# A two-layer expert kernel: bounds, probes and tally of the second layer's search re-ordered, and the first expert's weight splits moved past search phases

## The chip, the cores and the metric

The kernel runs on one core of a Trainium2 chip. The metric is the device time of one execution in microseconds (us); the median of the runs before the change is 927.05 us (three runs, 924.12 to 927.51). Besides these, one execution was profiled; it took 930.23 us, and its span from the first to the last instruction is 928.2 us.

## What is computed

Attention over q, k and v (batch 4, 12 heads, 448 tokens, width 64) gives 1792 rows of 768 numbers. Two expert layers follow. The first sends each row to its best expert by a gate. The second one is the subject here: every (row, expert) pair has a logit, the pairs are taken from the largest logit down, and an expert that has 224 rows is full.

```python
def _moe2_ref(x, w_gate, w1, w2) -> np.ndarray:
    N, D = x.shape
    E = w_gate.shape[1]
    cap = N // E
    logits = x @ w_gate
    flat = logits.flatten()
    order = np.argsort(-flat)
    assigned = -np.ones(N, dtype=np.int64)
    counts = np.zeros(E, dtype=np.int64)
    for idx in order:
        tok, e = (int(idx) // E, int(idx) % E)
        if assigned[tok] >= 0 or counts[e] >= cap:
            continue
        assigned[tok] = e
        counts[e] += 1
        if (assigned >= 0).all():
            break
    out = np.zeros((N, D), dtype=np.float32)
    for e in range(E):
        mask = assigned == e
        h = np.maximum(x[mask] @ w1[e], 0.0)
        out[mask] = h @ w2[e]
    return out.astype(np.float32)
```

## The kernel before

Matrix products are made of three TensorE (PE) products each: every fp32 operand is split into a high part (ScalarE copies it into fp32r) and a low part (VectorE subtracts), and high-high, high-low and low-high are added up.

The first layer's last block ends in `moe1` with lines 491 to 525. There the second layer's logits, all but the last block's, are loaded into `L`; `tail0` to `tail3` copy the last block's output, transpose it (`tail1`, whose second half VectorE copies into `yb`, L238), multiply it with the gate (`tail2`, L243) and transpose the logits back (`tail3`, L249, L250). Between them VectorE finds the smallest and largest logit (L503, L504), PE transposes the two numbers (L508), and VectorE makes 40 thresholds from them (L512 to L517). `warm` puts idle matmuls into PE's queue.

The second layer (`moe2`) doesn't sort. It finds one expert at a time: the generator `phases()` runs `search(p)` and `assign(p)`, and each `yield` ends a phase. One expert has 15:

- Phase 1 takes each row's best logit and compares it with 40 thresholds (`probe`, L680: 14 x 40 results a partition, `t_g`). Phases 2, 4, 6 and 8 count the rows over each threshold with 14 small matmuls (L723) and compare the counts with the capacity (L724, L728). Phases 3, 5 and 7 add up the comparisons with one matmul (L736), narrow the thresholds (L739) and probe again.
- Phase 9 takes the final threshold and tallies the rows over it by expert (L743 to L746, `tally`, `owned`). Phase 10 adds the tally up (L624), lowers the capacities and picks the full expert, whose number lets the SP queue load its weights (L753 to L767). Phases 11 to 15 make the list of its 224 rows: a running count, an offset matmul (L774), one-hot tables (L783 to L787), 14 matmuls on them (L791), the index matmul (L797) and the index list `idx` (L800). GpSimd then gathers the rows (`gather`, L849).

The order in which the queues get their work is written out in the program's text. Expert 0's search runs alone (`finish(0)`). After that `go(n)` runs n phases at once, while `turn`, called after each half of an up product and each pair of a down product, runs one when a countdown (the numbers `YY`) has run out. The first expert's head (L931 to L955) runs phases 1 to 5 of expert 1 between warm matmuls, then `take` transposes the rows, and then the loop over k = 0 to 5 makes the first four hidden slices (`up4`, L898), splits a chunk of w1 for k + 2 (`split`, L841 and L842) and calls `go(1)`:

```python
        for k in range(KD):
            if k:
                go(1)
            if k + 2 < KD:
                split(0, k + 2)
            up4(k, 0, 2)
            if k in (2, 3):
                go(1)
            up4(k, 2, 4)
```

So the loop holds phases 6 to 12. The next loop (L957 to L965) makes slices 4 to 7 (`up`, L891, 18 matmuls a slice), with `relu` (L903, L904) and the splits of the eight chunks of w2 in the order 0, 4, 1, 5, 2, 6, 3, 7. The down product (`down`, L914) follows in 16 pairs of slices; its first pair needs chunks 0 and 1, its second 2 and 3, its fourth 6 and 7. Weights come in a ring of eight buffers `raw`. The other seven experts run the same loops, with the next search in the turns.

## Time and profile before

| What | Value |
|---|---|
| median of three runs | 927.05 us |
| the profiled execution: its own time | 930.23 us |
| the profiled execution: its span | 928.2 us |
| PE busy | 872.0 us (94% of the span) |
| VectorE busy | 596.1 us (64%) |
| ScalarE busy | 478.7 us (52%) |
| GpSimd busy | 178.7 us (19%) |
| mean granted TensorE clock | 0.986 of full speed |

A busy share is a mean over stages that have different limits. In the trace the first layer ends near 582 us, the first search of the second layer lasts to about 603 us, the first expert's head to about 640 us, and the other experts fill the rest.

### The profile page before, as it was taken

The page shows a single profiled execution, that of the slowest core. Times are in us where ns is not written, and L with a number is a line of the kernel's source. Part 1 is how long each engine was busy: PE and PEld are TensorE (multiplying, and loading weights), DVE is VectorE, ACT ScalarE, POOL GpSimd, SP SyncE. Part 2 cuts the span into 40 slices and gives each one's busy share as a digit, 9 for nine tenths or more (in the row PEclk, how much of TensorE's full clock was granted, in tenths as well). Part 3 has the DMA queues.
Part 4 walks back from the last instruction along what each step waited for, and adds up shares of the span by engine and source line. Part 5 has one row for each costly group of instructions (what it writes and reads, how often), then busy time and mean ns, then how long its engine had stood idle before and what let it go on. Part 6 is the DMA issues. An engine that isn't in the chain of part 4 may idle for free. (4 is left out here: it accounts for less than half of the span.)

```text
span 928.2 us, 18427 instructions
## 1 busy us (share of the span) xinstructions
PE 872.0 (94%) x6380; PEld 726.8 (78%) x6380; DVE 596.1 (64%) x1749; ACT 478.7 (52%) x1042; POOL 178.7 (19%) x235
## 2 busy tenths in 40 slices
PE   7999999967999999798999999889999999999987
PEld 5666666646787887676888888468989999999987
DVE  7779898867463526738621241788888798875641
ACT  7777777765464526637722242035544354545541
POOL 6644444010111211110212120101011011011001
PEclk9999999989999999989999999999999999999999
DMA  7453537148374616837731111177575575666810
GB/s 177 120 150 103 149 102 227 51 129 295 127 275 134 237 54 216 337 109 284 281 99 35 54 38 41 58 262 227 190 234 187 161 235 177 220 195 195 263 51 30
DMA packets 73888, 151.05 MB, mean 163 GB/s; under 512 B 30481, under 2 KB 38705, under 8 KB 73714
## 3 DMA queue, kind: packets, MB, share of 16 engines
q1 hardware_dynamic: 67602, 123.33, 40.9%
q0 software_dynamic: 6112, 25.71, 8.4%
q8 instruction: 71, 1.16, 0.5%
q14 instruction: 103, 0.84, 0.3%
HBM read 130.34 MB, written 18.67 MB: 161 GB/s over the span
## 5 line engine op out<-in xcount | busy, mean ns | idle before, releaser
L206 PE MATMUL pU<-w1h,xx 128*128 128x512 f32 x336 | 119.1, 412 | 4.3 <-ACT yr L229 2.5
L891 PE MATMUL w<-xh,w1h 128*128 128x224 f32 x360 | 102.1, 284 | 0.7 <-ACTq L979 0.7
L891 PE MATMUL w<-xl,w1h 128*128 128x224 f32 x360 | 99.2, 276 | 1.2 <-issue 1.2
L891 PE MATMUL w<-xh,w1l 128*128 128x224 f32 x360 | 98.9, 275 | 0.6 <-DVEq L979 0.6
L1147 ACT ACTIVATE p<-p,nm 112x112 f32<-112x112 f32 (+2 forms) x192 | 98.8, 518 | 0.7 <-DVE nm L1139 0.7
L1139 DVE CUSTOM_DVE_ANT_0 p<-s,msk 112x112 f32<-112x112 f32 (+2 forms) x192 | 76.1, 445 | 23.6 <-PE s L1136 23.3
L914 PE MATMUL w<-w2h,hh 128*112 128x384 f32 x256 | 89.7, 350 | 0.1
L914 PE MATMUL w<-w2h,hl 128*112 128x384 f32 x256 | 86.5, 338 | 0.0
L914 PE MATMUL w<-w2l,hh 128*112 128x384 f32 x256 | 86.0, 336 | 0.0
L206 PEld LDWEIGHTS pU<-w1h,xx 128*128 128x128 f32 x336 | 63.7, 190 | 21.9 <-ACT yr L229 3.1
L891 PEld LDWEIGHTS w<-xl,w1h 128*128 128x128 f32 x360 | 69.1, 192 | 1.5 <-issue 1.4
L891 PEld LDWEIGHTS w<-xh,w1h 128*128 128x128 f32 x360 | 69.0, 192 | 1.4 <-ACTq L979 0.9
L891 PEld LDWEIGHTS w<-xh,w1l 128*128 128x128 f32 x360 | 69.1, 192 | 0.7 <-DVEq L979 0.7
L176 DVE TENSOR_TENSOR w2l<-raw,w2h 128x768 fp32r<-128x768 f32 x64 | 58.2, 954 | 17.1 <-ACT w2h L175 14.6
L224 PE MATMUL pY<-w2h,hh 128*128 128x384 f32 x224 | 60.7, 353 | 7.7 <-ACT w1h L175 5.0
L842 DVE TENSOR_TENSOR w2l<-raw,w2h 128x768 fp32r<-128x768 f32 x64 | 60.9, 952 | 8.6 <-ACT w2h L841 8.4
L206 PE MATMUL pU<-w1l,xx 128*128 128x512 f32 x168 | 66.1, 398 | 0.2 <-DVE w1l L441 0.2
L903 ACT ACTIVATE hh<-w 128x224 fp32r<-128x224 f32 x64 | 22.9, 358 | 82.0 <-PE w L891 56.3
L842 DVE TENSOR_TENSOR w1l<-raw,w1h 128x1024 fp32r<-128x1024 f32 x48 | 58.1, 1220 | 9.6 <-ACT w1h L841 9.4
L176 DVE TENSOR_TENSOR w1l<-raw,w1h 128x1024 fp32r<-128x1024 f32 x42 | 49.7, 1220 | 22.0 <-ACT w1h L175 22.0
L224 PE MATMUL pY<-w2h,hl 128*128 128x384 f32 x224 | 58.6, 343 | 1.0 <-DVE hl L217 1.0
L224 PE MATMUL pY<-w2l,hh 128*128 128x384 f32 x224 | 58.8, 345 | 0.0
(327 smaller groups left out, 2041.5 us busy)
## 6 DMA issues: line engine op xcount, KB each, us to landing
raw<-in_moe_w_dram SPq DMA_DIRECT2D x96, 512.0 KB
raw<-in_moe_w_dram SPq DMA_DIRECT2D x128, 384.0 KB
vt<-in_v_dram SPq DMA_DIRECT2D x48, 112.0 KB
qr<-in_q_dram SPq DMA_DIRECT2D x23, 224.0 KB
kr<-in_k_dram SPq DMA_DIRECT2D x23, 224.0 KB
xs<-xr SPq DMA_DIRECT2D x4, 1120.0 KB
xs<-xr SPq DMA_DIRECT2D x4, 238.0 KB
y<-yr SPq DMA_DIRECT2D x1, 384.0 KB
```

Of the source, the lines that this page charges most:

```text
L176: (on or nc.vector).tensor_sub(l, r, h.bitcast(F32))
L206: nc.tensor.matmul(pU[half], a[:, k], w[:, k, cs], start=(m == 0), stop=(m == 17))
L224: nc.tensor.matmul(pY[g][:, :384], a[:, k], w[:, k, g * 384:(g + 1) * 384], start=(k == 0 and t == 0), stop=(k == KF - 1 and t == 2))
L842: V.tensor_sub(l, r, h.bitcast(F32))
L891: nc.tensor.matmul(u, w[:, k, fs], x[:, k], start=(k == 0 and n == 0), stop=(k == KD - 1 and n == 2))
L903: A.activation(hh[:, f], u, AF.Relu)
L914: nc.tensor.matmul(y, a[:, f, g * G2:(g + 1) * G2], w[:, f, hf * 384:(hf + 1) * 384], start=(f == 0 and n == 0), stop=(f == KF - 1 and n = ...
L1139: nc.vector.tensor_tensor_reduce(P[u, h][:, o:o + w], s[h][:, :w], msk[:, S - w:], scale=-0.125, scalar=3.0e38, op0=OP.add, op1=OP.min, ac ...
L1147: nc.scalar.activation(p, p, AF.Exp, bias=RS[u, "m"][:, h, i:i + 1], scale=-1.0, accum_out=RS[u][:, h, i:i + 1])
```

## The change

Five places are edited. (1) At the end of the first layer the minimum and maximum are taken ahead of two other operations and written into `mn2`; the copy of `yb` follows them, and on PE the gate product of the last block stands ahead of the transposes of the bounds. (2) In expert 0's search, and there alone, the probe is two operations over 7 of 14 columns each, and the one-hot table stands ahead of the first probe. (3) The tally of phase 9 compares and multiplies in one operation, ahead of `asg` and `fl`; in phase 10 `mem` stands ahead of `ei`, and `fl` behind. Two warm matmuls behind expert 0's 14 index matmuls are gone. (4) An index list of zeros and one gather with it are issued ahead of expert 0's search. (5) In the head's loop `go(1)` is called at k = 4 and 5 and once behind the loop; it was called seven times.

```diff
-        V.tensor_tensor_reduce(d, d, hp, scale=-1.0, scalar=0.0, op0=OP.mult, op1=OP.add, accum_out=tk)
-        V.tensor_scalar(oi, iok[:, :NB], tk, None, op0=OP.is_equal)
-        V.tensor_reduce(d[:, 0:1], L, axis=AX.XY, op=OP.min)
-        V.tensor_reduce(d[:, 1:2], L, axis=AX.XY, op=OP.max)
-        tail1()
-        warm(2)
-        for n in range(2):
-            nc.tensor.transpose(pU[0][:, n * 128:n * 128 + 128], d[:, n:n + 1].to_broadcast([128, 128]), ident)
-        tail2()
+        V.tensor_reduce(mn2[:, 0:1], L, axis=AX.XY, op=OP.min)
+        V.tensor_reduce(mn2[:, 1:2], L, axis=AX.XY, op=OP.max)
+        tail1()
+        V.tensor_tensor_reduce(d, d, hp, scale=-1.0, scalar=0.0, op0=OP.mult, op1=OP.add, accum_out=tk)
+        V.tensor_scalar(oi, iok[:, :NB], tk, None, op0=OP.is_equal)
+        warm(2)
+        tail2()
+        for n in range(2):
+            nc.tensor.transpose(pU[0][:, n * 128:n * 128 + 128], mn2[:, n:n + 1].to_broadcast([128, 128]), ident)
         warm(2)
...
-        def probe():
+        def probe(parts=1):
 
-            V.tensor_tensor(T["g"][:, :, :TH], T["mm"][:, :, None].to_broadcast([128, PT, TH]),
-                            thr[:, None, :].to_broadcast([128, PT, TH]), op=OP.is_ge)
+            for i in range(parts):
+                s = slice(i * PT // parts, (i + 1) * PT // parts)
+                n = s.stop - s.start
+                V.tensor_tensor(T["g"][:, s, :TH], T["mm"][:, s, None].to_broadcast([128, n, TH]),
+                                thr[:, None, :].to_broadcast([128, n, TH]), op=OP.is_ge)
...
-                probe()
                 V.tensor_tensor(T["oh"], L, T["mm"][:, :, None].to_broadcast([128, PT, E]), op=OP.is_equal)
+                probe(2)
...
-                    probe()
+                    probe(1 if p else 2)
+            V.scalar_tensor_tensor(T["ao"], T["mm"][:, :, None].to_broadcast([128, PT, E]), thr[:, 0:1], T["oh"],
+                                   op0=OP.is_ge, op1=OP.mult)
+            with nc.allow_low_precision("small whole numbers"):
+                V.tensor_reduce(T["rab"], T["ao"].rearrange("p i e -> p e i"), axis=AX.X, op=OP.add)
             V.tensor_scalar(T["asg"], T["mm"], thr[:, 0:1], None, op0=OP.is_ge)
             V.tensor_scalar(T["fl"][:, 2:3], T["fl"][:, 2:3], float(PT), None, op0=OP.not_equal)
-            tally()
...
             V.tensor_reduce(T["em"], T["full"], axis=AX.X, op=OP.min)
-            V.tensor_scalar(T["fl"][:, :2], T["fl"][:, :2], 0.0, None, op0=OP.not_equal)
+            V.tensor_scalar(T["mem"], own, T["em"], None, op0=OP.is_equal)
             V.tensor_scalar(T["ei"], T["em"], 8.0, 7.0, op0=OP.add, op1=OP.min)
             EV[p] = nc.values_load(T["ei"][0:1, 0:1], engines=[SP], min_val=0, max_val=E - 1)
-            V.tensor_scalar(T["mem"], own, T["em"], None, op0=OP.is_equal)
             with nc.allow_low_precision("small whole numbers"):
                 V.tensor_reduce(T["rt"], T["mem"], axis=AX.X, op=OP.add)
+            V.tensor_scalar(T["fl"][:, :2], T["fl"][:, :2], 0.0, None, op0=OP.not_equal)
             yield YY[4]
...
             V.tensor_scalar(T["ev"], t[:16, :NA], float(N), None, op0=OP.min)
-            if p == 0:
-                warm(2)
             yield YY[9]
...
-        def gather(p):
-            for g in range(2):
+        def gather(p, n=2):
+            for g in range(n):
...
         reset()
+        nc.gpsimd.memset(idx[0], 0)
+        gather(0, 1)
         finish(0)
...
         for k in range(KD):
-            if k:
-                go(1)
             if k + 2 < KD:
                 split(0, k + 2)
             up4(k, 0, 2)
-            if k in (2, 3):
+            if k > 3:
                 go(1)
             up4(k, 2, 4)
+        go(1)
         ahead[0] = 1
```

How this moves instructions shows on VectorE, in three places. The first is the end of the first layer, before the change (`xg` holds `d`, `hp`, `tk` and `oi`; ISA is the multiply with a sum, L501):

```order
L500 SCALAR_TENSOR_TENSOR xg_3364<-xg_3364 128x128
L501 ISA xg_3364<-xg_3364 128x128
L501 ISA xg_3364 128x1
L502 TENSOR_SCALAR xg_3364<-iok_78,xg_3364 128x14
L503 TENSOR_REDUCE xg_3364<-L_82 128x1
L504 TENSOR_REDUCE xg_3364<-L_82 128x1
L238 COPY yb_3371<-pB1_3393 128x256
L512 TENSOR_REDUCE srch0_84<-pU0_3394 128x1
```

and with the change:

```order
L500 SCALAR_TENSOR_TENSOR xg_3364<-xg_3364 128x128
L501 TENSOR_REDUCE xg_3364<-L_82 128x1
L502 TENSOR_REDUCE xg_3364<-L_82 128x1
L238 COPY yb_3371<-pB1_3393 128x256
L504 ISA xg_3364<-xg_3364 128x128
L504 ISA xg_3364 128x1
L505 TENSOR_SCALAR xg_3364<-iok_78,xg_3364 128x14
L512 TENSOR_REDUCE srch0_84<-pU0_3394 128x1
```

The copy of `yb` has moved past three instructions, and they stand between it and the first operation on the transposed bounds (L512).

The second place is the head's loop, behind the three low parts of the gathered rows; before (`w1l` is the split of a w1 chunk, L724 and L728 belong to the even phases, L739 to the odd ones):

```order
L842 TENSOR_TENSOR w1l_23636<-raw2_90,w1h_23635 128x1024
L724 ISA t_d_23675,t_mx_23676<-gp_24062,t_capm_23667 40x8
L724 ISA t_mx_23676 40x1
L728 TENSOR_SCALAR t_ok_23677<-t_mx_23676 40x1
L732 ISA t_ao_23679,t_fl_23681<-t_oh_23673 128x112
L732 ISA t_fl_23681 128x1
L842 TENSOR_TENSOR w1l_23636<-raw3_91,w1h_23635 128x1024
L739 SCALAR_TENSOR_TENSOR srch3_87<-gp_24095,steps_23658,t_base_23696 128x40
L680 TENSOR_TENSOR t_g_23674<-t_mm_23670,srch3_87 128x14x40
L718 TENSOR_TENSOR t_col_23702<-srch3_87,steps_23658 128x1
L719 TENSOR_SCALAR t_base_23696<-iok_78,steps_23658,t_col_23702 128x40
L842 TENSOR_TENSOR w1l_23636<-raw4_92,w1h_23635 128x1024
```

and with the change:

```order
L846 TENSOR_TENSOR w1l_23636<-raw2_90,w1h_23635 128x1024
L846 TENSOR_TENSOR w1l_23636<-raw3_91,w1h_23635 128x1024
L846 TENSOR_TENSOR w1l_23636<-raw4_92,w1h_23635 128x1024
L846 TENSOR_TENSOR w1l_23636<-raw5_93,w1h_23635 128x1024
L727 ISA t_d_23675,t_mx_23676<-gp_24117,t_capm_23667 40x8
L727 ISA t_mx_23676 40x1
L731 TENSOR_SCALAR t_ok_23677<-t_mx_23676 40x1
L735 ISA t_ao_23679,t_fl_23681<-t_oh_23673 128x112
L735 ISA t_fl_23681 128x1
L742 SCALAR_TENSOR_TENSOR srch3_87<-gp_24147,steps_23658,t_base_23696 128x40
L683 TENSOR_TENSOR t_g_23674<-t_mm_23670,srch3_87 128x14x40
```

The last four splits of w1 stand in one run ahead of phase 6; before, the phases stood between them.

The third place is the end of the w2 splits; before, the one-hot tables of phase 13 (`t_a`, `t_b`) stood ahead of the first of the eight (chunk 0, `raw6`):

```order
L783 TENSOR_TENSOR t_a_23692<-t_ab_23691,ioi_23640 128x210
L785 TENSOR_TENSOR t_b_23693<-t_ab_23691,ioi_23640 128x224
L787 TENSOR_TENSOR t_a_23692<-t_a_23692,tok_23642 128x210
L904 SCALAR_TENSOR_TENSOR hl_23639<-w_24046,hh_23634 128x224
L842 TENSOR_TENSOR w2l_23638<-raw6_94,w2h_23637 128x768
L904 SCALAR_TENSOR_TENSOR hl_23639<-w_24212,hh_23634 128x224
L842 TENSOR_TENSOR w2l_23638<-raw2_90,w2h_23637 128x768
```

and with the change:

```order
L846 TENSOR_TENSOR w2l_23638<-raw1_89,w2h_23637 128x768
L783 COPY t_col_23702<-gp_24314 128x1
L785 SCALAR_TENSOR_TENSOR t_si_23690<-t_cum_23687,t_col_23702,t_mem_23686 128x14
L786 TENSOR_SCALAR t_ab_23691<-t_si_23690 128x14
L787 TENSOR_SCALAR t_ab_23691<-t_si_23690 128x14
L908 SCALAR_TENSOR_TENSOR hl_23639<-w_24291,hh_23634 128x224
L846 TENSOR_TENSOR w2l_23638<-raw5_93,w2h_23637 128x768
L789 TENSOR_TENSOR t_a_23692<-t_ab_23691,ioi_23640 128x210
L791 TENSOR_TENSOR t_b_23693<-t_ab_23691,ioi_23640 128x224
L793 TENSOR_TENSOR t_a_23692<-t_a_23692,tok_23642 128x210
L798 TENSOR_SCALAR t_ev_23694<-gp_24346 16x15
```

Phase 12 now stands ahead of the last w2 split (chunk 7, `raw5`) and phase 13 behind it. On PE the 14 index matmuls of phase 14 stand behind the third pair of the down product, and the index matmul of phase 15 behind the fourth.

## Rows read from the trace of the kernel before

**Rows 1.** Busy time by stretch: start:end, length, busy time (count) of PE, PEld, DVE, ACT, POOL, granted clock, DMA.
```profile
612.70:626.80 14.10, 12.39 (x105) 11.41 (x105) 12.16 (x46) 5.41 (x8) 0.00 (x0) 0.88 0.68 239
...
626.80:640.00 13.20, 13.20 (x113) 12.73 (x111) 11.71 (x31) 7.60 (x15) 2.52 (x6) 1.00 0.70 213
...
640.00:888.00 248.00, 245.27 (x2012) 231.50 (x2011) 191.20 (x552) 116.66 (x187) 27.24 (x26) 1.00 0.64 205
```

**Rows 2.** Timeline of PE around the bounds: start, us, engine, line, operation, idle before.
```profile
582.32 0.93 PE L233 MATMUL pB<-ident,yr 128*128 128x128 f32 x6 [0.72 <-ACT yr L229]
...
583.75 0.50 PE L508 MATMUL pU<-ident,xg 128*128 128x128 f32 x2
...
584.18 0.42 PE L243 MATMUL pA<-hb,wg 128*32 128x128 f32 x8
...
584.74 0.60 PE L488 MATMUL pU<-iob,before 128*128 128x512 bf16 x2
```

**Rows 3.** Timeline of VectorE around the bounds.
```profile
583.79 0.41 DVE L238 COPY yb<-pB 128x256 f32<-128x256 f32 x1
...
584.36 0.29 DVE L512 TENSOR_REDUCE srch<-pU 128x1 f32<-128x128 f32 x1 [0.15 <-PE pU L508]
...
585.67 0.18 DVE L250 TENSOR_REDUCE l2c<-pA 128x8 f32<-128x32 f32 x1
```

**Rows 4.** Timeline of VectorE in one round of the first search and at its end.
```profile
589.94 0.74 DVE L680 TENSOR_TENSOR t_g<-t_mm,srch 128x560 bf16<-128x560 f32 x1
...
590.60 0.15 DVE L718 TENSOR_TENSOR t_col<-srch,steps 128x1 f32<-128x1 f32 x1
...
591.29 0.16 DVE L724 CUSTOM_DVE_ANT_0 t_d<-gp,t_capm 40x8 f32<-40x8 f32 x1 [0.19 <-PE gp L723]
...
601.61 0.17 DVE L792 TENSOR_SCALAR t_ev<-gp 16x15 f16<-16x15 f32 x1 [0.59 <-PE gp L791]
```

**Rows 5.** Timeline of PE in the same round and at the same end.
```profile
590.74 0.51 PE L723 MATMUL gp<-t_oh,t_g 128*40 128x8 bf16 x14 [0.16 <-DVE t_g L680]
...
591.18 0.60 PE L594 MATMUL w<-iob,before 128*128 128x512 bf16 x2
...
602.04 0.21 PE L797 MATMUL gp<-t_ev,sel 16*112 16x15 f16 x1
```

**Rows 6.** Timeline of GpSimd: the second layer's first and second gathers.
```profile
603.59 1.13 POOL L849 DMA_INDIRECT xg<-y,idx  x1 [16.80 <-issue]
...
633.41 1.22 POOL L849 DMA_INDIRECT xg<-y,idx  x1 [27.23 <-DVE hl L904]
```

**Rows 7.** Timeline of PE in the first expert of the second layer.
```profile
626.81 0.28 PE L891 MATMUL w<-xh,w1h 128*128 128x224 f32 x1
...
629.71 0.27 PE L891 MATMUL w<-xl,w1h 128*128 128x224 f32 x1
...
638.96 0.34 PE L914 MATMUL w<-w2h,hh 128*112 128x384 f32 x1
...
641.00 0.51 PE L723 MATMUL gp<-t_oh,t_g 128*40 128x8 bf16 x14 [0.82 <-DVE t_g L680]
```

**Rows 8.** Timeline of VectorE in the first expert of the second layer.
```profile
620.33 0.26 DVE L739 SCALAR_TENSOR_TENSOR srch<-gp,steps,t_base 128x40 f32<-128x40 f32 x1 [0.27 <-PE gp L736]
...
621.83 1.22 DVE L842 TENSOR_TENSOR w1l<-raw,w1h 128x1024 fp32r<-128x1024 f32 x1
...
625.58 0.16 DVE L777 COPY t_col<-gp 128x1 f32<-128x1 f32 x1 [1.19 <-PE gp L774]
...
627.14 0.38 DVE L904 SCALAR_TENSOR_TENSOR hl<-w,hh 128x224 fp32r<-128x224 f32 x1
...
637.53 0.95 DVE L842 TENSOR_TENSOR w2l<-raw,w2h 128x768 fp32r<-128x768 f32 x1
```

**Rows 9.** Busy time by stretch around two idle times of PE, columns as in rows 1.
```profile
622.00:625.00 3.00, 3.00 (x16) 3.00 (x16) 2.36 (x14) 0.00 (x0) 0.00 (x0) 0.50 0.36 112
...
889.00:893.00 4.00, 1.75 (x11) 1.38 (x11) 1.35 (x2) 1.09 (x2) 0.00 (x0) 1.00 0.27 82
```

More of the change, by code (lines that the diff above doesn't have):

```diff
@@ L494, in moe1 @@
         V = nc.vector
-        d, hp, rh, oi, tk = xg[:, :128], xg[:, 128:256], xg[:, 256:256 + NB * E], xg[:, 512:512 + NB], xg[:, 640:641]
+        d, hp, rh, oi, tk, mn2 = xg[:, :128], xg[:, 128:256], xg[:, 256:256 + NB * E], xg[:, 512:512 + NB], xg[:, 640:641], xg[:, 648:650]
         V.tensor_copy(tk, sin)
```

## The prediction, made before the changed kernel was run

> **What bounds the kernel now.** I read the page's busy shares first (TensorE, PE, has work in 94% of the span), then the busy times by stretch, then the timelines of PE, VectorE and GpSimd where the change acts. From 640 us on PE is busy for 245.27 of 248 us [rows 1]: nothing there absorbs or adds, so a shift of the first expert's down product reaches the end of the kernel whole. The change acts between 582 and 640 us. In the head's loop (612.7 to 626.8) PE is busy for 12.39 of 14.10 us at a granted clock of 0.88, VectorE for 12.16; in the stretch behind it PE for all of 13.20 us and VectorE for 11.71 [rows 1]. The reader should see two engines that are both nearly full: VectorE is idle for only 1.94 + 1.49 = 3.43 us of 27.3. Shortening PE's loop helps only until VectorE decides.
>
> **End of the first layer (edit 1).** Before, the transposes of the bounds start at 583.75 and the gate product (0.42 us) follows at 584.18 [rows 2]; VectorE's first reduction of the bounds (L512) waits 0.15 us for PE and then runs on without a wait up to the copy of the logits (L250, 585.67) [rows 3]. Now the gate product comes first. It needs the copy of `yb` (L238, at 583.79, 0.41 us [rows 3]), whose source is done at 582.32 + 0.93 = 583.25 [rows 2]. Before, the copy stood behind four operations that are now behind it or already done; now it can take 583.3 to 583.7, and the gate product starts at about 583.75, where the bounds started. It holds PE for 0.56 us (584.18 to 584.74, its start to the next operation's [rows 2]). The bounds follow 0.56 us later, and since L512 to L250 have no slack, so does the search: **+0.56**. Were the logits the last thing to come, the earlier gate product would give back at most 584.18 - 583.75 = 0.43. As L250 shows no wait, I take +0.56 and keep -0.43 as the other end.
>
> **First search (edits 2 and 3).** A probe of 560 elements takes 0.74 us, with the next operation 0.66 us after its start [rows 4]; an operation of 224 elements takes 0.38 with the next one 0.30 on [rows 8]. Between them lies 280 elements: 0.44, the next 0.36 on. Two halves take 0.72 of VectorE's time, not 0.66: +0.06 a round. PE's 14 counting matmuls take 0.44 (590.74 to 591.18 [rows 5]) after the whole probe; now seven of them run beside the second half, and 0.22 is left behind it, 0.22 - 0.06 = 0.16 earlier. VectorE waited 0.19 us for them (591.29 [rows 4]), which with its 0.06 leaves at most 0.13. Three rounds give **-0.4**; the first probe gives nothing, because the one-hot table, which the matmuls need too, moved ahead of it. The ends are -0.5 (0.16 x 3) and +0.25 (four times 0.06, if the matmuls wait for both halves; the order of the program puts their second wait at the eighth).
>
> A rule speaks against halves. The Trainium skill, page "VectorE: DVE Perf Modes", section "The TRN2 errata — SBUF-src ops pay a fixed extra latency per instruction", says that many small tiles pay a fixed cost each, and gives some 150 cycles at 0.96 GHz. By that four more instructions would be an estimated +0.6 us, and the search would come out 0.5 worse than in my sum. The rows show a start-to-start fixed part of about 0.06 (the pair 224/0.30 and 560/0.66), because the next instruction starts before the last one ends.
>
> The fused tally takes out one operation of VectorE and changes no dependence that PE waits on: 0 (to -0.28, the length of such an operation in the loop). In phase 10 `mem` goes ahead of `ei`: -0.05 (to -0.14); the expert's number comes 0.06 later, and its loads have slack. The two warm matmuls stood between the index matmuls and the index product: `ev` ends at 601.61 + 0.17 = 601.78 [rows 4] and the product starts at 602.04 [rows 5]; it can start at 601.84: **-0.2**. Together the first search comes to +0.56 - 0.4 - 0.05 - 0.2, about **-0.1**.
>
> **Gather of row zero (edit 4).** GpSimd is idle for 16.80 us ahead of the real gather at 603.59, whose issue takes 1.13 us [rows 6]. The extra gather is one more such issue in that idle time, into a buffer that the real one overwrites, so it hides; cost without cover would be 1.13. If a first issue is slower than later ones, it could take that off the real gather: 603.59's 1.13 is no longer than the second one's 1.22 [rows 6], so I take 0 (-0.3 to +1.1).
>
> **The head's loop (edit 5).** Four calls of a phase leave the loop; it keeps phases 6, 7 and 8. PE's 1.71 us without work go, and the 3 us at clock 0.50 (622 to 625 [rows 9]) cost about 1.7 that a full clock saves; the wait inside phase 8 is kept (+0.4), the small matmuls of four phases go (-0.6): the loop ends about **3.6 us earlier**, at 623.2 instead of 626.8. That isn't a gain yet, because the same VectorE work must still be done. I follow its chain. Slice 4's 18 matmuls (0.11 each: 27 from 626.81 to 629.71 make 2.90 [rows 7]) end at 625.2; the first `hl` and the phases that now come with the turns follow at about 625.6. From there on VectorE has, in one run: phase 9 1.50 (620.33 to 621.83); seven pairs of `hl` and split, 0.30 + 0.87 each, 8.2; phases 10 and 11 1.42 (end of the split at 621.83 + 1.14 to 625.58, less the wait of 1.19); phases 12 and 13 1.56 (625.58 to 627.14) [rows 8]. That is 12.7, and the last split ends at 638.3; before it ended at 637.53 + 0.95 = 638.48 [rows 8]. **So of 3.6 us, 0.2 survive on VectorE.**
>
> PE pays the rest by waiting: about 1.8 us ahead of the second pair of the down product, for the split of chunk 3 (done near 635.5, wanted near 633.7), and 1.3 ahead of the 14 index matmuls of phase 14, which need the tables of phase 13 that now stand behind the last split. Then come phase 14 (0.54), the fourth pair of slices (1.05, half of 638.96 to 641.0 without its wait [rows 7]) and the index product with its wait (0.35): the fifth pair starts near 640.3. Before, the point that answers to it is the end of the counting matmuls at 641.00 + 0.44 = 641.4 [rows 7], which holds phase 2 of expert 2 (0.55 with its wait shortened) that now comes later. The gain is 641.4 - 0.55 - 640.3 = 0.6: **-0.6** (0 to -3.6).
>
> The gather for expert 1 moves from 633.41 to about 641, the searches of all later experts run four turns later; the gathered rows are wanted only at expert 1's start, far behind.
>
> **Sum.** -0.1 and -0.6: -0.7. The profiled execution took 930.23 us, so 929.5 by its own time. It lies 3.18 above the median of 927.05; against that median I forecast **926.3**.
>
> **The rivals.** *The loop's gain is kept* (0.22): VectorE's idle 3.43 us close up, because its operations run closer together when they stand in a run, and both pairs come as early as PE's loop allows. -3.6 and -0.1: 923.4. For it: the splits overlap PE work in either order. Against it: 638.3 against 638.48 above.
>
> *Slower: the clock falls* (0.20). PE has worked without a pause from 626.8 to 640 [rows 1]; in the new order it waits for about 3.1 of the 4.6 us from 633.7 to 638.3. Such a thinned stretch inside the loop left a clock of 0.50 over 622 to 625 [rows 9]. If the same follows here, some 3.4 us of products run at half rate, worth 1.7: -0.7 + 1.7 = +1.0, 928.0. [...] Against it: from 889 to 893 PE is busy for 1.75 of 4 us at clock 1.00 [rows 9]. The Trainium skill, page "TensorE: Matmul & The Clock Gate", section "What's actually happening", says that the throttled clock is the default and that activity releases it; by that the fall is what idling invites, and the two stretches of rows 9 bear it out once and not the other time.
>
> *Expert 1 starts late* (0.06): its gather sits at 641 behind GpSimd's own work, and four chunk loads behind the late number; PE then waits some 4 us at the next head: 931.
>
> **How the numbers follow.** The forecast has 0.50, with 924.7 to 928.7 as its own range (the ends of the first layer's and of the probe's terms, and 1.0 for the median of a few runs). The range reaches from somewhat below the first rival (923.4 less the 1 us) to somewhat above the second (928.0 and 1.7): 922.4 to 929.7. About 0.5%, 4.6 us, is what a measurement of this kernel can tell from no change; that is under 922.4 or over 931.7. Half of the first rival (0.11: it lies 1 us from that bound) and 0.02 of the forecast's lower end make faster 0.13; the third with a trace of the second makes slower 0.07; 0.80 stays.
>
> **What would show it.** Right: L512 starts near 584.9; the second probe half overlaps counting matmuls; the index product starts within 0.1 us of `ev`; the loop ends 3 to 4 us earlier; PE waits for `w2l` at the second pair and for phase 13 at the third; the fifth pair starts near 640. Wrong: no wait of PE between 633 and 639 (first rival), a granted clock under 0.9 from 633 to 642 (second), or PE waiting at expert 1's transposes (third). A gather whose issue or landing becomes shorter than before would show that edit 4 was worth something.

## The result, and the profile after

The change is slower. Its median is 933.91 us (eight executions, 929.35 to 936.53) against 927.14 for the kernel before: a ratio of 1.0068, 95% interval 1.0043 to 1.0094. Timed again it came to 932.86 against 928.17, 1.0054 (1.0031 to 1.0078). The forecast was 926.3, with 922.4 to 929.7 as its range. The profiled execution took 936.12 us with a span of 934.3. PE is busier than before, in the same share of the span, so nothing there tells why (first part of the page, changed kernel):

```profile
PE 876.3 (94%) x6378; PEld 729.4 (78%) x6378; DVE 597.3 (64%) x1753; ACT 478.5 (51%) x1042; POOL 178.7 (19%) x237
```

What does tell is the busy time by stretch, in the columns of [rows 1]: first the head's loop, then the first down product, then expert 1's head.

```profile
612.04:622.40 10.36, 9.91 (x102) 9.27 (x101) 8.17 (x16) 5.70 (x8) 0.00 (x0) 1.00 0.75 250
...
637.00:640.00 3.00, 2.39 (x20) 2.14 (x20) 0.72 (x3) 0.00 (x0) 0.00 (x0) 0.50 0.69 280
640.00:643.00 3.00, 3.00 (x10) 2.63 (x10) 2.30 (x13) 1.43 (x2) 1.00 (x2) 0.50 0.00 0
...
660.00:663.00 3.00, 2.41 (x10) 2.14 (x10) 2.13 (x8) 0.00 (x0) 0.34 (x1) 0.52 0.77 213
663.00:666.00 3.00, 3.00 (x15) 2.79 (x15) 2.37 (x6) 1.09 (x2) 0.00 (x0) 0.50 0.48 168
```

The loop takes 10.36 us where it took 14.10 [rows 1], 3.7 less, at a clock of 1.00. But behind it the granted clock stands at 0.50 (the lower of its two levels, 1.2 of 2.4 GHz) twice, where the kernel before had 1.00 from 626.8 to 888 [rows 1]. PE's waits in the same places, from its timeline (start, us, engine, line, operation, idle before):

```profile
634.95 0.43 PE L918 MATMUL w<-w2l,hh 128*112 128x384 f32 x1 [1.80 <-DVE w2l L846]
...
658.02 0.51 PE L726 MATMUL gp<-t_oh,t_g 128*40 128x8 bf16 x14 [1.06 <-DVE t_g L683]
...
662.22 0.55 PE L895 MATMUL w<-xl,w1h 128*128 128x224 f32 x1 [0.49 <-DVE xl L884]
```

The number in brackets is PE's idle time before the operation and what ended it. The first is the forecast wait for the split of chunk 3; another of 0.77 us, ahead of phase 14, follows at 637.61. The second pair of waits was not forecast: it stands at expert 1's head, where the kernel before has no wait of PE. Behind it is ScalarE, which waits there for weights to arrive:

```profile
650.64 1.06 ACT L845 ACTIVATE w1h<-raw 128x1024 fp32r<-128x1024 f32 x1 [3.11 <-DMA raw<-in_moe_w_dram]
...
654.17 1.06 ACT L845 ACTIVATE w1h<-raw 128x1024 fp32r<-128x1024 f32 x1 [2.10 <-DMA raw<-in_moe_w_dram]
```

And behind that GpSimd, whose timeline shows expert 1's gather, and after it four one-element memsets on the weight buffers. These are fences: four weight loads (chunks 2 to 5 of expert 1's w1) are issued only after them.

```profile
641.70 0.94 POOL L853 DMA_INDIRECT xg<-y,idx  x1 [38.77 <-DVE t_m L675]
642.94 1.32 POOL L853 DMA_INDIRECT xg<-y,idx  x1 [0.30 <-issue]
644.25 0.18 POOL L1066 MEMSET raw<- 1x1 f32 x4
```

The gather was at 633.41 before [rows 6], 51.1 us after the transposes of [rows 2] began; now it is 61.9 us after the same point (59.2 in a second trace of the change). In the waits of the SP queue (line, what it waited for, us in total, times, longest) from 600 to 662 us the fences held the queue for 10.0 us, in one piece:

```profile
SPq L832 <- POOL raw L1066: 10.0, 1, 10.0
```

### The profile page after: what moved, and what is told of

Same layout as the page of the kernel before. It is cut to its first block, busy times and chain, and to the rows that moved or that the text cites. A ratio compares the mean times of both kernels' runs of the same rounds, so it can differ in the third digit from the quotient of the medians.

```text
span 934.3 us, 18424 instructions
## 1 busy us (share of the span) xinstructions
PE 876.3 (94%) x6378; PEld 729.4 (78%) x6378; DVE 597.3 (64%) x1753; ACT 478.5 (51%) x1042; POOL 178.7 (19%) x237
## 5 line engine op out<-in xcount | busy, mean ns | idle before, releaser
L845 ACT ACTIVATE w1h<-raw 128x1024 fp32r<-128x1024 f32 x48 | 48.3, 1053 | 25.9 <-DMA raw<-in_moe_w_dram 25.5
```

Of the source, the lines that this page charges most:

```text
L845: A.activation(h, r, AF.Copy)
```

## The experiments

Each was compared with the kernel before, run on the same chip. "Starts" are counted from the first transpose of the first layer's last output (L233: 582.32 before [rows 2], 579.85 in the changed kernel), because that point moves by some us from execution to execution.

### The loop or the other four edits

The loop alone in the kernel before, and the changed kernel with the old loop:

```diff
         for k in range(KD):
-            if k:
-                go(1)
             if k + 2 < KD:
                 split(0, k + 2)
             up4(k, 0, 2)
-            if k in (2, 3):
+            if k > 3:
                 go(1)
             up4(k, 2, 4)
+        go(1)
```

> The kernel before, with the head's loop of the change (edit 5) and nothing else. Three theories of the +6.3 us (927.1 to 933.9 and the profile's granted clock of 0.50 at 606 to 609, 636 to 644 and 660 to 667). Clock theory: the two waits of PE in the first down product (1.80 and 0.77 us) let the clock fall, 2.5 us there and some 4 us at the next expert's head: 932 to 935, with the clock at 0.50 behind the waits. Late-list theory: expert 1's index list comes 7 us later, so its gather and four chunk loads come late and PE waits at expert 1's head: the same time here. Other-edits theory (edits 1 to 4 cost, by the fall at 606 to 609): 927 to 929, and the loop alone is worth little.

Measured: 933.87 us, 1.0049 (1.0025 to 1.0073), as slow as the whole change; its trace has the clock at 0.50 from 610 to 613 and behind the first waits.

> The changed kernel with the head's loop as it was before (edits 1 to 4 kept). Clock and late-list theories: 926 to 928, as the kernel before, since only the loop made the waits. Other-edits theory: 931 to 934, with the clock at 0.50 at 606 to 609.

Measured: 927.35 us, 0.9981 (0.9963 to 0.9998). The loop is the cause; edits 1 to 4 cost nothing. (With the new loop they show no gain either: 1.0049 without them, 1.0054 and 1.0068 with them.) Its trace has the clock at 1.00 through the whole of 580 to 700 us, so it will serve as the mark for what follows.

### PE's first waits: filled

```diff
-                        down(g, hf, f, f + 2)
+                        if p == 0 and n == 1:
+                            down(g, hf, f, f + 1)
+                            warm(8)
+                            down(g, hf, f + 1, f + 2)
+                        else:
+                            down(g, hf, f, f + 2)
+                        if p == 0 and n == 2:
+                            warm(4)
                         turn(p, 1)
```

> The changed kernel with idle matmuls where PE waits in the first expert's down product: 8 (1.7 us) between slices 2 and 3, 4 (0.85 us) ahead of phase 14. No work comes earlier by this. Clock theory: the clock stays at 1.00 from 633 to 645, the fifth pair comes about 2.5 us earlier, and the time falls by 2 to 5 us, to 929 to 932. Late-list theory: the list stays late, the waits at expert 1's head stay or grow, 932.5 to 934.5.

Measured: 931.24 us, 1.0025 (1.0009 to 1.0041). The stretch that stood at 0.50 (windows, same columns):

```profile
637.00:640.00 3.00, 2.87 (x28) 1.97 (x26) 1.67 (x5) 0.00 (x0) 0.00 (x0) 1.00 0.84 328
640.00:643.00 3.00, 3.00 (x18) 2.75 (x17) 2.36 (x13) 1.44 (x2) 1.05 (x2) 1.00 0.10 36
```

The clock holds behind the waits (at 606 to 609 this trace has the fall too), and over its twelve executions the mean granted clock is 0.988, against 0.984 over the change's first eight and 0.986 over the kernel before on this chip. The fifth pair comes 1.0 us earlier after L233 than in the change's first trace, not 2.5 (59.57 against 60.57), and the waits at expert 1's head are still there, 1.20 and 1.19 us. Of the +0.68% some 0.3 to 0.4 went, the rest stayed.

With idle matmuls in the head too:

```diff
-        warm(7)
+        warm(11)
         go(1)
-        warm(2)
+        warm(4)
         split(0, 0)
```

> The changed kernel with the two filled waits and idle matmuls also ahead of the first two small products of the head (4 and 2 more), where PE waits 1.01 and 0.62 us and the clock stood at 0.50 from 606 to 609 in all four kernels profiled with the new loop, and in neither with the old one. If PE's idle time there makes the fall, the head is 1.8 us shorter: 929 to 930. If the fall comes from elsewhere (or falls only in some executions), 930.5 to 931.5.

Measured: 932.21 us, 1.0027 (1.0009 to 1.0045), the same as without them; no fall in its head, and nothing won. One trace without a fall doesn't show that the filling prevents it: other traces with these waits empty have none either. The fall at 606 to 609 lies ahead of the new loop's waits; it is taken up again below.

### The search ahead of the splits

```diff
             up(f, 0)
-            turn(0, 1)
+            go(1)
+            flush()
             relu(f - 4)
             split(0, KD + f - 4)
             up(f, 1)
-            turn(0, 1)
+            if f < KF - 1:
+                go(1)
+            flush()
```

> The changed kernel with one phase after each half of slices 4 to 7, so that phases 9 to 15 of expert 1 are done ahead of the down product, as before the change; VectorE's amount of work is the same, so the last w2 split stays near 638. Late-list theory: the gather comes near 632, the four loads near 637, expert 1's head starts without a wait: 927 to 930. Clock theory: PE's waits move to the w2 splits (one of them 1.8 to 3 us), the clock still falls behind them, and the time stays 931 to 934.

Measured: 931.05 us, 1.0020 (1.0001 to 1.0039). Both parts of the expectation came in half: the waits at expert 1's head are gone, but PE waits 2.77 us for phase 13 between slices 6 and 7, the clock stands at 0.50 behind it, and expert 1 begins at +79.81, later than in the change (+78.98). VectorE's work doesn't shrink by being re-ordered; a wait of PE only moves.

### The late loads

```diff
                             if p == 0:
-                                for _, k in pend:
-                                    nc.gpsimd.memset(raw[(NC + k) % NR][:1, :1], 0.0)
-                                lim[0] = 1
                                 flush()
...
-        lim, done, wait, pend, pace, ahead = [0], [], [0], [], [1], [2]
+        lim, done, wait, pend, pace, ahead = [1], [], [0], [], [1], [2]
```

With the waits filled as well:

> The changed kernel with the two waits of the first down product filled by idle matmuls (as in the run before) and, besides, the four loads of expert 1's w1 chunks 2 to 5 no longer held behind its gather (their fences on GpSimd are gone). Late-list theory as the second half of the cost: the loads start some 3 us earlier, ScalarE's two waits for weights at expert 1's head (3.1 and 2.1 us in the changed kernel) shrink, PE's waits there (1.2 and 1.2 us) go, and the time falls by a further 1.5 to 2.5 us, to 928.5 to 930. If the lateness of the list itself is what counts (the gather, not the loads), the time stays at 931.

Measured: 929.16 us, 1.0000 (0.9983 to 1.0016).

By itself:

> The changed kernel with nothing but the four loads of expert 1's w1 chunks 2 to 5 freed from their fences behind the gather; PE's waits in the first down product stay empty. With the two kernels before (filled: +0.25% against the kernel before; filled and early loads: 0.00%; the change +0.68%) this closes a square. If the two costs add up, the early loads alone take off the same 0.25 points: about +0.4%, 931 to 932.5 where the kernel before takes 928.5. If the fall of the clock hides the loads' lateness (PE is slow and wants its weights later), they give less than 0.1 points: 933 to 934.

Measured: 929.28 us, 1.0002 (0.9980 to 1.0024): a miss, for the expectation from separate costs was +0.4%, and it stands level with the run that has the waits filled as well. PE's first waits are still there, 1.79 and 1.01 us, and in this trace the clock stayed at 1.00 behind them. That left open whether the loads had brought the falls, so change and early loads were run once more, together on one chip:

> The changed kernel once more, beside the kernel with the early loads and on the same chip: +0.4 to +0.8% against the kernel before, mean granted clock some 0.002 under that of the kernel before, and a fall to 0.50 behind the first waits in the trace. If +0.68% came of the chip, it is under +0.3% here.

> The changed kernel with the early loads and nothing else, once more: 0.0 to +0.2%. If the loads' lateness is a cause by itself, it stays at least 0.3 points under the change on the same chip whether or not the clock falls behind the first waits (1.8 and 1.0 us), which are still there; a fall in this trace would say that the fall is the chance of an execution and that PE's second waits are the loads' part. No fall and the same mean clock as the kernel before would say that the late loads bring the falls too.

Measured: the change 932.86, 1.0054 (1.0031 to 1.0078); with early loads 930.76, 1.0020 (1.0000 to 1.0039), 0.34 points less, or 3.2 us (the medians lie 2.1 apart, and the two intervals overlap). The fall that was expected in the change's trace is missing: neither trace has a fall between 580 and 700 us, though both have the same first waits, so these two show the loads' price alone. Over the twelve executions of each the mean clock is the same, 0.9842 and 0.9843, and under the kernel before's 0.9861 on this chip, so in this pair it isn't the late loads that bring it down (the first run with early loads had 0.9867). PE's timeline of the change (first transpose, second down pair, phase 14, fifth down pair, the waits at expert 1's head, the last expert's first product):

```profile
582.51 0.93 PE L233 MATMUL pB<-ident,yr 128*128 128x128 f32 x6 [0.72 <-ACT yr L229]
...
635.94 0.42 PE L918 MATMUL w<-w2l,hh 128*112 128x384 f32 x1 [1.80 <-DVE w2l L846]
...
638.60 0.50 PE L797 MATMUL gp<-t_a,t_b 128*16 128x15 f16 x14 [1.01 <-DVE t_a L793]
...
640.40 0.43 PE L918 MATMUL w<-w2h,hh 128*112 128x384 f32 x1
...
657.14 0.51 PE L726 MATMUL gp<-t_oh,t_g 128*40 128x8 bf16 x14 [1.37 <-DVE t_g L683]
...
661.33 0.38 PE L895 MATMUL w<-xl,w1h 128*128 128x224 f32 x1 [1.19 <-DVE xl L884]
...
890.32 0.35 PE L895 MATMUL w<-xh,w1h 128*128 128x224 f32 x1
```

and with the early loads, where the waits at expert 1's head shrink to 0.15 us:

```profile
581.25 0.93 PE L233 MATMUL pB<-ident,yr 128*128 128x128 f32 x6 [0.72 <-ACT yr L229]
...
634.67 0.43 PE L918 MATMUL w<-w2l,hh 128*112 128x384 f32 x1 [1.80 <-DVE w2l L846]
...
639.13 0.43 PE L918 MATMUL w<-w2h,hh 128*112 128x384 f32 x1
...
657.19 0.38 PE L895 MATMUL w<-xl,w1h 128*128 128x224 f32 x1 [0.15 <-DVE xl L884]
...
886.20 0.35 PE L895 MATMUL w<-xh,w1h 128*128 128x224 f32 x1
```

The fifth pair starts at 640.40 - 582.51 = 57.89 and at 639.13 - 581.25 = 57.88: up to there the two are one. The last expert starts at 307.81 and 304.95. **The late loads cost 2.86 us**, waits of PE at expert 1's head and what follows from them: the two traces are alike up to there, and these waits are 2.56 us in the one and 0.15 in the other.

Two controls in the kernel before. First the loads freed there:

> The kernel before with the four loads freed from their fences. In its trace expert 1's head has no wait of PE, so by the late-list theory nothing is to be had: 928 to 929, within 0.1% of the kernel before. If the loads run into the gather and make it late, it is slower by up to 2 us.

Measured: 928.88 us, 0.9991 (0.9973 to 1.0009): nothing to be had, as expected. Then the loads made late there:

```diff
-                        if p + 1 in done and not early:
+                        if p + 1 in done and not early and (p or n >= 3):
+                            if p == 0:
+                                nc.gpsimd.tensor_copy(raw[(NC + pend[0][1]) % NR][:1, :1], yo[:1, 0, :1])
                             gather(p + 1)
```

> The kernel before with its old loop, but with expert 1's gather made to wait on GpSimd for the first output half of the down product (a copy of one number of it), so that the gather and the four fenced loads come at about 641 to 644, as in the change, instead of 633 to 638. Late-list theory: ScalarE waits for w1 at expert 1's head, PE waits there 1 to 2.5 us, and the time rises by 0.2 to 0.6%, without any of the loop's changes. If the waits in the down product are needed for the cost, it stays within 0.1% of the kernel before.

Measured: 929.05 us, 1.0001 (0.9981 to 1.0020): a miss. GpSimd's and ScalarE's timelines say why:

```profile
639.89 0.18 POOL L1063 MEMSET raw<- 1x1 f32 x4
```
```profile
645.91 1.06 ACT L841 ACTIVATE w1h<-raw 128x1024 fp32r<-128x1024 f32 x1 [2.06 <-DMA raw<-in_moe_w_dram]
...
648.20 1.06 ACT L841 ACTIVATE w1h<-raw 128x1024 fp32r<-128x1024 f32 x1 [0.19 <-DMA raw<-in_moe_w_dram]
```

Counted from L233 the fences come even later than in the change (639.89 - 577.26 = 62.63 against 644.25 - 582.51 = 61.74). What differs is their lead over the rows' first transposes (`take`), whose operands share ScalarE and VectorE with these splits. Here the transposes start at 647.86, 7.97 us behind the fences; in the change's second trace at 650.34, 6.09 us behind 644.25; in the kernel before the last of the four fences (638.59) is 13.08 us ahead of them (651.67). This run, the change, the kernel before:

```profile
647.86 0.60 PE L876 MATMUL w<-ident,xg 112*128 112x112 f32 x4
```
```profile
650.34 0.60 PE L880 MATMUL w<-ident,xg 112*128 112x112 f32 x4
```
```profile
638.59 0.09 POOL L1061 MEMSET raw<- 1x1 f32 x1 [1.13 <-issue]
```
```profile
651.67 0.60 PE L876 MATMUL w<-ident,xg 112*128 112x112 f32 x4
```

So the loads came late here too, but with 1.9 us more lead: ScalarE waits 2.06 and 0.19 us, not 3.94 and 1.58 as in that trace of the change, and PE hardly at all (0.22). The experiment left the loads just enough lead. It doesn't speak against the loads in the change, but it shows no cost without the loop either.

### PE's second waits: filled

```diff
                         down(g, hf, f, f + 2)
+                        if p == 0 and n == 15:
+                            warm(5)
                         turn(p, 1)
...
                     up(f, 0)
                     turn(p, 1)
+                    if p == 1 and f == 0:
+                        warm(5)
                     up(f, 1)
```

> The changed kernel with idle matmuls at expert 1's head alone: 5 (1.07 us) ahead of the last small product before its first up product, and 5 between the halves of that up product. The first waits stay empty and the loads stay late, so no work comes earlier. If the clock's falls come from the second waits as much as from the first, the time falls by 2 to 3 us from the change's +0.68%, to about +0.3 to +0.4%, and the mean granted clock rises from 0.984 to 0.987. If only the first waits make falls, the time stays at +0.5 to +0.7% and the clock at 0.984.

Measured: 933.30 us, 1.0038 (1.0021 to 1.0054), mean clock 0.984. The time fell by as much as was expected, but the clock didn't rise: behind the first waits, which stay empty here, it still stood at 0.50.

```profile
637.00:640.00 3.00, 2.43 (x21) 1.89 (x21) 1.56 (x5) 0.00 (x0) 0.00 (x0) 0.50 0.88 343
640.00:643.00 3.00, 3.00 (x10) 2.42 (x9) 1.49 (x9) 1.44 (x2) 0.46 (x1) 0.50 0.01 4
```

The intervals of this run and of the change overlap, so the gain of the second filling is not settled: the time agrees with the one theory of the expectation, the clock with the other.

### Fewer phases moved, and the old loop with its waits filled

The old loop, with idle matmuls in front of its four waiting products, and in the head the 4 and 2 of the run above:

```diff
             if k:
+                if k in (3, 5):
+                    warm(2)
                 go(1)
...
             if k in (2, 3):
+                warm(3 if k == 2 else 1)
                 go(1)
```

> The changed kernel with the old loop (927.35 in the run before), and idle matmuls in the waits of the head and of the loop (0.64, 0.44, 0.46 and 0.49 us). Clock theory: where falls to 0.50 come in some executions (clock 0.982 to 0.986 in half of the runs), they go, so the median moves to that of the undisturbed ones, 925.5 to 927, with a smaller spread. If the falls don't depend on these waits: 927 to 928.

Measured: 927.02 us, 0.9968 (0.9951 to 0.9984), **the lowest ratio of all**, below the kernel before and the change; no fall of the clock in its trace from 580 to 920 us. It lies on the border of the two expectations, and its interval overlaps that of the old loop without idle matmuls (0.9963 to 0.9998), so what the filling adds isn't settled.

Two phases moved out of the loop, with and without edits 1 to 4 (the diff is against the change):

```diff
             up4(k, 0, 2)
-            if k > 3:
+            if k > 1:
                 go(1)
```

> The changed kernel with phases 6 to 10 in the loop, so that two phases leave it and not four. The total of VectorE's work is the same, and the list comes two turns earlier than in the change. Both theories: smaller waits in the down product and at expert 1's head, 928 to 931, between the old loop's 927.4 and the change's 933.9. If it were under 926.5, the loop's gain would be real and the change only overdid it.

> The kernel before with phases 6 to 10 in the loop and nothing else. If the loop with two phases moved is a gain by itself: 926 to 927.5 where the kernel before takes 928.5. If edits 1 to 4 made the -0.25% (with the old loop they gave -0.19%), this equals the kernel before: 928 to 929.

Measured: 926.79, 0.9975 (0.9960 to 0.9990) with the other edits, a miss to the good side (928 to 931 was expected) that isn't told apart from the old loop's 0.9981; 928.67, 0.9997 (0.9975 to 1.0019) without them. Two phases moved are no gain by themselves. The first of these with the head's waits filled, the early loads, and idle matmuls ahead of phase 15:

```diff
             yield YY[9]
+            if p == 1:
+                warm(3)
             t = small(16)
```

> The changed kernel with phases 6 to 10 in the loop (two moved: -0.25% against the kernel before), with the early loads and with idle matmuls in the head's waits and ahead of phase 15. If the two costs are all that stands against moving phases, this is the fastest: 924.5 to 926.5, -0.3 to -0.5%. If two phases moved leave no such cost, it equals the two moved: 926 to 927.5.

Measured: 927.84, 0.9985 (0.9964 to 1.0006), no better, and above both of its expectations.

## Why the prediction was wrong, step by step

**The bounds: right in place, free in the end.** The timeline of PE in the changed kernel has the gate product ahead of the bounds:

```profile
579.85 0.93 PE L233 MATMUL pB<-ident,yr 128*128 128x128 f32 x6 [0.72 <-ACT yr L229]
...
581.25 0.43 PE L243 MATMUL pA<-hb,wg 128*32 128x128 f32 x8
...
581.82 0.43 PE L509 MATMUL pU<-ident,xg 128*128 128x128 f32 x2
```

The bounds start 1.97 us after L233 where it was 583.75 - 582.32 = 1.43 [rows 2]: +0.54, forecast +0.56. The first counting matmuls came only 0.20 later (586.14 - 579.85 = 6.29, before 588.41 - 582.32 = 6.09): 0.34 of it was given back by then.

**The halves and the tally.** A round of the first search, from one narrowing product to the next on PE:

```profile
589.50 0.17 PE L739 MATMUL gp<-t_ok,ones 40*128 40x1 bf16 x1
...
591.67 0.17 PE L739 MATMUL gp<-t_ok,ones 40*128 40x1 bf16 x1
```

2.17 us, where the kernel before has 591.72 - 589.45 = 2.27: -0.10 a round, forecast -0.13. On VectorE the two halves take 0.81 us together, the whole took 0.74 [rows 4]: +0.07, forecast +0.06.

```profile
590.00 0.81 DVE L683 TENSOR_TENSOR t_g<-t_mm,srch 128x280 bf16<-128x280 f32 x2
```

By the page cited there (the Trainium skill, "VectorE: DVE Perf Modes", section "The TRN2 errata — SBUF-src ops pay a fixed extra latency per instruction", some 150 cycles at 0.96 GHz) the second half would have cost an estimated 0.16 more; the trace shows 0.07. The tally gave another -0.2, forecast 0. Phase 10 took that back: its offset product now waits 0.37 us for `rt`, forecast -0.05. Without the two warm matmuls the index product starts 0.76 us after the index matmuls instead of 0.97 (599.61 - 598.85, 602.04 - 601.07), the forecast -0.2; but the index matmuls start 0.19 later after the offset product. Together the head's first product starts at 30.51 us after L233 (613.03 - 582.51, in the second trace of the change), before at 30.39 (612.71): +0.1, forecast -0.1.

**The gather of row zero.** The real gather's issue starts 600.54 - 599.61 = 0.93 us after the index product, before 603.59 - 602.04 = 1.55 [rows 5, 6], and takes 0.93 us, not 1.13. No product of PE came earlier for it: 0, as forecast.

**The loop: the schedule was right, the account wrong.** The loop became 3.7 us shorter (forecast 3.6), PE waited 1.80 us for chunk 3 (1.8) and 1.01 for phase 14 (1.3), and the fifth pair started at 57.89, forecast 640.3 - 582.32 = 57.98. Two steps failed. One is the credit: 1.7 of the 3.6 us were the clock of 0.50 over 622 to 625 [rows 9], taken as something that the new loop removes; the old loop with edits 1 to 4 runs without that fall too (below). The other is that a shift of the down product "reaches the end of the kernel whole", with "the gathered rows are wanted only at expert 1's start, far behind" as all that was said of the four later turns. What that left out cost three things.

First, **the loads**: the forecast followed the gather, and named the four loads behind it only in the third rival (0.06, 931). That rival was right in its mechanism and nearly in its size: 2.86 us of 4.

Second, **the products and waits that left the loop come back later**. The sum took off 0.6 us for the small products of four phases in the loop and gave back one phase, 0.55; of the waits it gave back 1.8 and 1.3 in the first down product and none behind. With early loads the last expert starts at 304.95; with the old loop and the same edits it starts at 885.52 - 582.11 = 303.41. Busy time by stretch, columns as in [rows 1], for the head, for the loop with slices 4 to 7, for the first down product up to expert 1's first product, and for the rest up to the last expert. The old loop with edits 1 to 4:

```profile
582.11:612.62 30.51, 25.97 (x217) 12.80 (x217) 25.49 (x119) 3.92 (x7) 6.98 (x30) 1.00 0.45 151
612.62:634.52 21.90, 19.91 (x192) 18.50 (x192) 19.86 (x62) 11.63 (x20) 2.08 (x2) 1.00 0.66 217
634.52:656.57 22.05, 21.22 (x170) 19.09 (x168) 18.23 (x52) 9.93 (x15) 1.40 (x6) 1.00 0.69 227
656.57:885.52 228.95, 226.96 (x1859) 215.13 (x1857) 177.41 (x514) 107.07 (x174) 25.62 (x24) 1.00 0.67 206
```

and the new loop with early loads:

```profile
581.25:611.76 30.51, 25.97 (x217) 12.78 (x217) 25.51 (x119) 3.92 (x7) 6.97 (x30) 1.00 0.46 153
611.76:630.89 19.13, 18.68 (x177) 17.76 (x177) 15.84 (x46) 11.68 (x20) 0.00 (x0) 1.00 0.47 163
630.89:655.24 24.35, 21.54 (x171) 19.15 (x169) 20.66 (x59) 9.87 (x15) 3.33 (x3) 1.00 0.78 270
655.24:886.20 230.96, 228.03 (x1873) 215.51 (x1872) 179.17 (x523) 107.20 (x174) 26.62 (x24) 1.00 0.65 204
```

The clock is 1.00 in all eight. PE's work is the same in sum, 294.05 and 294.21 us: the 1.23 us that leave the second stretch come back, 0.32 in the third and 1.07 in the fourth, not the one phase of the sum. PE's idle time (the length less the busy time) falls by 1.54 in the second stretch, and grows by 1.98 in the third and 0.94 in the fourth. **The loop by itself is worth +1.54 us, not -0.6**. The forecast of -0.6 was counted from the trace of the kernel before, which has a fall in the second stretch:

```profile
612.71:635.80 23.09, 21.38 (x192) 20.12 (x192) 19.77 (x62) 11.64 (x20) 2.08 (x2) 0.93 0.64 214
...
657.84:886.68 228.84, 226.93 (x1859) 215.11 (x1857) 176.66 (x514) 107.16 (x174) 25.64 (x24) 1.00 0.65 206
```

There the last expert starts at 886.68 - 582.32 = 304.36. Even against that the new loop is 0.59 later, with its loads early, and 3.45 later with them late.

Third, **the clock**: the second rival (0.20, priced 1.7 us). Where it falls it costs more: the change's first trace has falls, its second has none, and the last expert starts at 893.37 - 579.85 = 313.52 in the one and at 307.81 in the other, 5.7 us later; 1.7 of them are from the fall at 606 to 609, ahead of the loop. It doesn't fall in every execution: of the seven traces in which PE's first waits are empty (the change twice, early loads twice, the loop alone, the search first, the second waits filled) four have the fall and three have not (in the search first, the wait and the fall stand further ahead). Over whole executions the mean clock tells more than a single trace: it was 0.9872 to 0.9878 in the three kernels with the first waits filled, and 0.9841 to 0.9850 in six of the seven runs with them empty (0.9867 in the first run with early loads). The change's twenty executions have 0.9843, the old loop with edits 1 to 4 has 0.9872. Among those twenty, an execution with a mean clock 0.001 lower took about 0.7 us longer (a straight line through them), so the 0.0029 are an estimated 2.0 us on average. The mean covers the whole kernel, the fall at 606 to 609 too, so this isn't the price of the first waits alone.

The Trainium skill, page "TensorE: Matmul & The Clock Gate", section "What's actually happening", has the throttled clock as the default, which activity releases. The traces agree on one side: with the first waits filled, the clock stayed at 1.00 behind them in all three. With the waits empty it was at 0.50 in four and at 1.00 in three, and the rule as cited doesn't say which.

**The sum as measured.** From the old loop with edits 1 to 4, which stands at -0.19%, that is -1.7 us (-3.4 to -0.2 by the interval): the loop 1.5, the loads 2.9, the clock an estimated 2.0 on average. That makes +6.4, and +4.7 us against the kernel before. The change measured +5.0 and +6.3 us; 4.7 is inside both intervals (from 2.9 and 4.0 us up). The loads are read from two traces that agree to 0.01 us up to the waits at expert 1's head. The two traces of the loop differ in the loads too, but freeing them under the old loop was worth nothing (0.9991). The clock's share is the least certain of the three.

**What stays open.** A fall in the head (606 to 609 in the change's first trace, up to 610 to 613 in others) came in seven traces out of thirteen with four or two phases moved, and in none of five with the old loop, though it lies ahead of the loop and filling the waits there gained nothing. Where edits 1 to 4 win their 0.2% can be placed: the head doesn't start earlier, but from the head's first product to the first down product the old loop takes 21.90 us with them and 23.09 in the kernel before, where the clock falls. The traces of the old loop with the old tally all have a fall to 0.50 inside the loop ([rows 9], and the two controls of the late loads), the two with the new tally have none; whether the tally or another edit keeps the clock up there was not tried by itself.

## What to carry to other kernels

When a producer is moved later, follow every queue that it feeds, down to the loads that are fenced behind it: here a list that came 8 us later cost nothing on the engine that made it and 2.9 us at the next expert's start, where the loads behind it had 6.1 us of lead; with 8.0 us of lead they made PE wait for 0.22. Work that leaves a busy stretch of the bounding engine for another busy stretch of the same engine is no gain; count it where it lands. A fall of the clock that one trace shows isn't yet the property of a stretch: before crediting an edit with its end, see whether the same stretch has it without the edit. And an engine that waits more in one place can pay again in its clock behind it: idle matmuls in the wait raised the mean clock again, but the order that didn't wait was faster.

## What was not expected of the hardware

The clock behind one and the same wait (1.80 and then 0.77 to 1.01 us) stood at 0.50 in one execution of the change and at 1.00 in another, and the falls came in company: of the seven traces with these waits empty, the four with a fall behind them are the four with a fall in the head, some 30 us earlier. And cutting an operation of 560 elements into two of 280 cost VectorE no more than 0.07 us: the round became 0.10 us shorter.
